# DMA transposes for q and k of batch 1 and for x of batches 2 and 3, and zero matmuls at the start, in a windowed-attention and gated-FFN kernel

## The chip, the cores and the metric

The kernel runs on one core of a Trainium2 chip. The metric is the device time of one execution in microseconds. Before the change the median of three runs is 214.59 us (213.76 to 214.88).

## The reference

Attention with a window of 128 and 4 sink keys for 4 batches of 8 heads, 768 positions and 64 elements per head. Its output, the heads side by side, is x (3072 tokens of 512), the input of a gated feed-forward part without a nonlinearity.

```python
scores = scale * np.matmul(q, k.transpose(0, 1, 3, 2))
is_sink = pos[None, :] < int(n_sink)            # n_sink 4
rel = pos[:, None] - pos[None, :]
in_window = (rel >= 0) & (rel < int(window))    # window 128
scores = np.where(is_sink | in_window, scores, -1000000000.0)
...
x = np.matmul(softmax(scores), v)    # then to 3072 x 512
a = x @ w1                           # 512 x 1024
b = x @ w2
h = a * b @ w3                       # 1024 x 1024
return (h @ w_out).astype(np.float32)   # 1024 x 512
```

## The kernel before, in words

**Attention.** A batch is cut into three stages t of 256 queries, and its 8 heads into four pairs r. For each batch q and k lie in SBUF with the tokens on the partitions (qN, kN) and must be transposed so that the head elements lie on the partitions (qT, kT). A batch has six key blocks kb of 128 tokens. `transposes` (L163) does two blocks with 8 TensorE transposes into one PSUM bank and one VectorE copy; `transposes_dma` (L175) does one block with one DMA transpose issued from SP. The set XPOSE (L54) says which batches take the second way: 2 and 3. `scores` (L216) makes the scores of one pair and stage (6 matmuls, or 4 for t = 0), ScalarE takes the exponential (L227), VectorE the mask (L231). `values` (L237) multiplies with v, and VectorE divides by the sum and writes xn (L259). `x_transposes` (L263) turns two pairs of xn into xT with 4 TensorE transposes and one ScalarE copy (L271).

**Feed-forward.** w3 and w_out are multiplied once (`fold_w3`, `fold_mm`, L297 to L317). `gate` (L277) makes a 128-column part of x @ w1 (half 0, copied out by ScalarE to a_sb) or of x @ w2 (half 1, multiplied by a_sb on VectorE into ab), 4 matmuls each, for a chunk of 256 tokens (batch 0) or 384 tokens (the others). `project` (L319) makes 128 rows of the result with 8 matmuls of 512 columns; ScalarE copies it to o_sb (L327), and SP issues the output (L330). The tile o_sb comes from the pool `work`, with 3 buffers.

**Queues.** All loads of inputs and weights are issued by POOL (L101, L104, L108) in the order of the list `order` (L124), with the type changed to bf16 on the way; for each batch and block k, q and v. SP issues the DMA transposes and the outputs. Each engine works through its own list in order. A load into a qN or kN buffer has to wait until that buffer's user of two batches before is done.

**Order.** TensorE, ScalarE, VectorE and SP have their order written out by a planner that runs while the kernel is built (L437 to L534). Tasks have stages (engine and assumed duration), predecessors (`after`), loads with assumed arrival times (L342) and a priority; `pe_pick` (L448) takes the task that can start first on TensorE, and the least priority number among those that needn't wait. The planner models the PSUM banks ("mm" with 4, "sc" with 2), but no buffer of the pool `work` and no sharing of the DMA engines: a DMA transpose is put at 1.4 us of SP and 6.5 us to landing (L381), an output at 0.1 us of SP (L433).

```python
task(qk[-1], 1, transposes_dma(src, dst, kb), [("sp", 1.4), ("dma", 6.5)],
     war, [(n, b, kb)])
```

Of the kernel before, what the change touches and what calls it, by code (L numbers as in the profile page):

```python
# [21 lines left out]
def kernel(  # L22
# [13 lines left out]
    nc = tc.nc  # L36
    FP32 = mybir.dt.float32
    BF16 = mybir.dt.bfloat16
# [4 lines left out]
    B, H, S, D = q.shape  # L43
    assert (B, H, S, D) == (4, 8, 768, 64)
    P = 128
    NP = H // 2
# [4 lines left out]
    KFF = DF // P  # L51

    CHUNKS = [[(256 * i, 256 * i + 256) for i in range(3)]] + [[(0, 384), (384, 768)]] * (B - 1)
    XPOSE = (2, 3)  # L54
    scale = 1.0 / float(D) ** 0.5

    const = ctx.enter_context(tc.tile_pool(name="const", bufs=1))
# [2 lines left out]
    work = ctx.enter_context(tc.tile_pool(name="work", bufs=3))  # L60
# [4 lines left out]
    ident = const.tile([P, P], BF16, name="ident")  # L65
# [5 lines left out]
    w3_sb = wp.tile([P, KFF, DF], BF16, name="w3_sb")  # L71
    wo_sb = wp.tile([P, KFF, DM], BF16, name="wo_sb")
    w3o = wp.tile([P, KFF, DM], BF16, name="w3o")
    VS = 80

    def per_batch(name, shape, bufs):
        return [inp.tile(shape, BF16, tag=f"{name}{b % bufs}", bufs=1, name=f"{name}_{b}")
# [48 lines left out]
             ("w3", 6, 8), ("qkv", 1, 0, 6), ("qkv", 2, 0, 6), ("qkv", 3, 0, 6)]  # L126

    nc.scalar.preload_act_table_set("natural_log_exp_and_others")
    nc.vector.memset(ident[:], 1.0)
    load(*order[0])  # L130
    nc.gpsimd.affine_select(ident[:], ident[:], compare_op=ALU.is_equal, fill=0.0,
# [24 lines left out]
    for x in order[4:]:  # L156
        load(*x)
    for b in range(B):
        nc.vector.memset(ksbd[b][:], 0.0)
        nc.vector.tensor_copy(vs[b][:, :, D], ones_s[:])  # L160


# [72 lines left out]
    xns = {}  # L235

    def values(b, r, t):  # L237

        am = ams.pop((b, r, t))
        av = ps_mm.tile([P, 2, 2, D + 1], FP32, tag="mm", name="av")  # L240
        todo = []
        for i in range(2):
            if t > 0:
                q0 = (t - 1) * 256 + i * P
                todo.append((av[:, i, :, :].rearrange("p e d -> p (e d)"), es[b][:, q0:q0 + P],
                             vs[b][:, 2 * r:2 * r + 2, :].rearrange("p e d -> p (e d)")))
            for kb, c in ((2 * t + i - 1, 2 * i * P), (2 * t + i, (2 * i + 1) * P)):
                if kb >= 0:
                    for e in range(2):
                        todo.append((av[:, i, e, :], am[:, e, c:c + P],  # L250
                                     vN[b][:, kb, 2 * r + e, 0:D + 1]))
        for n, (o, lhs, rhs) in enumerate(todo):
            nc.tensor.matmul(o, lhs, rhs, start=(n == 0), stop=(n == len(todo) - 1),  # L253
                             skip_group_check=True)
        yield
        rec = work.tile([P, 2, 2, 1], FP32, tag="rec", name="rec")
        nc.vector.reciprocal(rec[:], av[:, :, :, D:D + 1])  # L257
        xn = work.tile([P, 2, 2, D], BF16, tag="xn", bufs=4, name="xn")
        nc.vector.tensor_mul(xn[:], av[:, :, :, 0:D], rec[:].to_broadcast([P, 2, 2, D]))  # L259
        xns[b, r, t] = xn  # L260
        yield

    def x_transposes(b, r0, t):  # L263

        xt = ps_mm.tile([P, 2, 2, P], BF16, tag="mm", name="xt")
        for r in range(2):
            xn = xns.pop((b, r0 + r, t))
            for i in range(2):
                nc.tensor.transpose(xt[:, r, i, :], xn[:, i, :, :].rearrange("p e d -> p (e d)"), ident[:])  # L269
        yield  # L270
        nc.scalar.copy(xT[b][:, r0:r0 + 2, t * 256:(t + 1) * 256],  # L271
                       xt[:].rearrange("p r i m -> p r (i m)"))
        yield

    gate_a = {}
# [43 lines left out]
    def project(b, m):  # L319

        po = ps_mm.tile([P, DM], FP32, tag="mm", name="po")
        for kk in range(KFF):
            nc.tensor.matmul(po[:], ab[b][:, kk, m * P:(m + 1) * P], w3o[:, kk, :],  # L323
                             start=(kk == 0), stop=(kk == KFF - 1))
        yield
        o_sb = work.tile([P, DM], FP32, tag="o_sb", name="o_sb")
        nc.scalar.copy(o_sb[:], po[:])  # L327
        yield
        t0 = b * S + m * P
        nc.sync.dma_start(out=out[t0:t0 + P, :], in_=o_sb[:])  # L330
        yield


    arrive = {}
# [37 lines left out]
    for b in range(B):  # L372
        for t in range(NT):
            kbs = (2 * t, 2 * t + 1)
            qk = []
            war = [("av", b - 2, NP - 1, NT - 1)] if b >= 2 else []
            for n, src, dst in (("k", kN[b], kT[b]), ("q", qN[b], qT[b])):
                if b in XPOSE:
                    for kb in kbs:
                        qk.append(("tp" + n, b, kb))  # L380
                        task(qk[-1], 1, transposes_dma(src, dst, kb), [("sp", 1.4), ("dma", 6.5)],  # L381
                             war, [(n, b, kb)])
                else:
                    qk.append(("tp" + n, b, t))
                    task(qk[-1], 1, transposes(src, dst, t), [("pe", 0.48), ("dve", 0.62)],
                         war, [(n, b, kb) for kb in kbs], "mm")
            if t == 0:
                qk0 = qk
                task(("sk", b), 0, sink_keys(b), [("dve", 0.2)], [("sc", b, 1, 0)])
                task(("sv", b), 2, sink_values(b), [("pe", 0.3), ("act", 0.5)],  # L390
                     [("av", b - 2, NP - 1, NT - 1)] if b >= 2 else [], [("v", b, 0)], "mm")
            else:
                task(("ss", b, t), 2, sink_scores(b, t), [("pe", 0.5), ("act", 0.4)],
                     qk + [("sk", b)], ring="mm")
            for r in range(NP):
                after = list(qk)
                if b >= 2 and t == 0:
                    after.append(("g", b - 2, len(CHUNKS[b - 2]) - 1, KFF - 1, 1))
                lead = r % 2 == 0
                task(("sc", b, r, t), 4 if lead else 0, scores(b, r, t),  # L400
                     [("pe", 0.22), ("act", 0.83), ("dve", 0.58)] if t == 0 else
                     [("pe", 0.28), ("act", 1.05), ("dve", 0.7)], after, ring="sc",
                     slots=2 if lead else 1,
                     started=([("sc",) + unit[-1]] if unit else [])
                     + ([("av",) + unit[-3]] if lead and len(unit) > 3 else []))
                task(("av", b, r, t), 3, values(b, r, t),
                     [("pe", 0.2 if t == 0 else 0.37), ("dve", 0.55)],
                     [("sc", b, r, t)] + ([("ss", b, t), ("sv", b)] if t else []),
                     [("v", b, kb) for kb in kbs], "mm",
                     [("av",) + unit[-1]] if unit else [])  # L410
                unit.append((b, r, t))
                if not lead:
                    task(("xt", b, r - 1, t), 2.5, x_transposes(b, r - 1, t),
                         [("pe", 0.24), ("act", 0.6)],
                         [("av", b, r - 1, t), ("av", b, r, t)], [], "mm",
                         [("xt",) + unit[-4][:1] + (unit[-4][1],) + unit[-4][2:]] if len(unit) > 3 else [])
    gates = []
    for b in range(B):
        for c, (t0, t1) in enumerate(CHUNKS[b]):
            last_t = (t1 - 1) // 256  # L420
            us = 0.01 + 0.65 * (t1 - t0) / 384
            for dt in range(KFF):
                n = dt * P // 512
                pr = 1000 + 200 * b + 10 * c + dt
                war = [("p", b - 2, NB - 1)] if b >= 2 else []
                task(("g", b, c, dt, 0), pr + 0.5, gate(b, c, dt, 0), [("pe", us), ("act", 0.2 + us / 2)],
                     [("xt", b, NP - 2, last_t)] + war, [("w1", n), ("w2", n)], "mm",
                     [("g",) + gates[-2] + (1,)] if len(gates) > 1 else [])
                task(("g", b, c, dt, 1), pr, gate(b, c, dt, 1), [("pe", us), ("dve", 0.23 + us / 2)],
                     [("g", b, c, dt, 0)], ring="mm", half=True)  # L430
                gates.append((b, c, dt))
            for m in range(t0 // P, t1 // P):
                task(("p", b, m), 1300 + 200 * b + m, project(b, m), [("pe", 1.75), ("act", 0.6), ("sp", 0.1)],  # L433
                     [("g", b, c, KFF - 1, 1), ("fm", KFF - 1, 0), ("fm", KFF - 1, 1)], ring="mm")
# [4 lines left out]
    URGENT = {"g": 0, "av": 0, "sc": 2}  # L439
    PACE = 5.0  # L440
    last_sc = 0.0
    BACKLOG = 1.6
    free = {"pe": 0.0, "act": 0.0, "dve": 0.0, "sp": 0.0}
    rings = {n: [[0.0] for _ in range(k)] for n, k in (("mm", 4), ("sc", 2))}
# [54 lines left out]
    with tc.manual_schedule(engines={mybir.EngineType.PE, mybir.EngineType.Activation,  # L499
                                     mybir.EngineType.DVE, mybir.EngineType.SP}):  # L500
        while len(done) < len(tasks):
# [13 lines left out]
            start, _, e = min(moves)  # L515
            if e == "pe":
                k = pe[1]
                begun.add(k["name"])
                k["stage"] = 0
                us = k["stages"][0][1]  # L520
# [8 lines left out]
                queue[e].remove(q)  # L529
                us, k = q[2], q[3]  # L530
            next(k["gen"])
            if e == "pe" and start - free[e] > 0.3: print("model idle", k["name"], round(start,2), round(start - free[e],2))
            free[e] = start + us
            advance(k, free[e])  # L534

# [33 lines left out]
```

The softmax here doesn't subtract the row's maximum and nothing guards it: scores larger than these inputs give would overflow.

## Time and profile before

| | |
|---|---|
| median of three runs | 214.59 us |
| the profiled execution | 214.53 us |
| its span, first to last instruction | 212.8 us |
| TensorE busy | 195.3 us, 92% |
| VectorE, ScalarE busy | 109.5 us, 110.4 us |
| POOL busy (issuing loads) | 75.0 us, the last load issued at 98.5 us |
| mean granted TensorE clock | 0.989 |
| chain that ended last | PE 86%, POOL 5%, DMA 3%, DVE 3% |
| gate matmuls (L284) in that chain | 41% |
| projections (L323) in that chain | 20% |
| TensorE transposes (L168 and L269) in that chain | 4% |

A share of busy time is a mean over the whole span. The start, to about 27 us, has idle TensorE while weights and the first batch arrive; the middle, to about 117 us, has TensorE and the DMA engines both full; after that the DMA engines carry little but the outputs. The chain lists, followed back from the last instruction, what each step waited for. The prediction below quotes the lines it rests on: slices, the chain in order of time, and the timelines of POOL and SP, whose columns are the start in us, the time taken in us, the engine, the line, the operation, what it writes and reads, and in brackets what it waited for.

### The profile page before, as it was taken

Reading aid. Unit: us, or ns where it says so; the run is one execution under the profiler, and the core shown is the slowest. Engines: PE = TensorE matmul, PEld = TensorE weight load, DVE = VectorE, ACT = ScalarE, POOL = GpSimd, SP = SyncE. Lnnn points to the kernel's source line nnn. Section 1 sums busy time; section 2 is a strip of 40 time slices with the busy share of each in tenths; the row PEclk is TensorE's granted clock in tenths of the full one; section 3 lists DMA queues with packets and bytes.
Section 4 is the critical chain, followed back from the end, with each engine's and each line's share of the span. In section 5 each row is a group of like instructions: output and inputs, shape, how many; then the busy total and the mean of one; then the engine's idle time right before and its main releaser. Section 6 shows DMA issues by size and latency. Waiting matters only on the chain.

```text
span 212.8 us, 4647 instructions
## 1 busy us (share of the span) xinstructions
PE 195.3 (92%) x1888; PEld 131.8 (62%) x1888; DVE 109.5 (51%) x258; ACT 110.4 (52%) x197; POOL 75.0 (35%) x97
## 2 busy tenths in 40 slices
PE   0287799999998999999999999999999999999993
PEld 0266468998987887666666555666664466554441
DVE  7116825836697787776776444687740044440000
ACT  2012636644866686786666766766643333323332
POOL 7996573679999665666000000000000000000000
PEclk9999969999999999999999999999999999999998
DMA  4999999999999999999996222100002310002343
GB/s 65 160 170 205 165 198 204 163 178 157 156 155 132 156 156 149 136 154 146 140 117 124 102 107 93 49 2 3 0 3 99 148 49 3 2 0 99 152 162 133
DMA packets 96710, 24.43 MB, mean 115 GB/s; under 512 B 88496, under 2 KB 92592, under 8 KB 96688
## 3 DMA queue, kind: packets, MB, share of 16 engines
q0 software_dynamic: 80176, 14.69, 89.5%
q1 hardware_dynamic: 16512, 9.44, 21.3%
q8 instruction: 15, 0.25, 0.5%
q14 instruction: 7, 0.06, 0.1%
HBM read 29.36 MB, written 6.29 MB: 168 GB/s over the span
## 4 chain that ended last, share of the span: by engine, by line
PE 86%; POOL 5%; DMA 3%; DVE 3%; issue 1%; ACT 1%; POOLq 0%; ACTq 0%; DVEq 0%
PE pg L284 41%; PE po L323 20%; PE av L253 7%; PE sc L222 6%; PE pw L313 6%; DMA w_sb<-in_moe_w_dram 3%; PE xt L269 3%; PE sp L202 2%; PE tp L168 1%; POOL vN_90 L101 1%; POOL qN_82 L101 1%; DVE xn L259 1%; POOL kN_86 L101 1%; DVE am L231 1%; POOL w_sb L108 1%
## 5 line engine op out<-in xcount | busy, mean ns | idle before, releaser
L284 PEld LDWEIGHTS <-w_sb 128*128 128x128 bf16 x576 | 54.2, 99 | 27.6 <-issue 3.4
L227 ACT ACTIVATE ex<-sc 128x1024 bf16<-128x1024 f32 (+1 forms) x48 | 44.3, 955 | 13.3 <-PE sc L222 13.0
L291 ACT COPY a_sb<-pg 128x384 f32<-128x384 f32 (+1 forms) x72 | 32.1, 446 | 34.2 <-PE pg L284 20.0
L231 DVE TENSOR_TENSOR am<-ex,maskt 128x1024 bf16<-128x1024 bf16 (+1 forms) x48 | 30.4, 643 | 10.0 <-ACT ex L227 9.0
L327 ACT COPY o_sb<-po 128x512 f32<-128x512 f32 x24 | 14.0, 585 | 27.2 <-PE po L323 24.8
L284 PE MATMUL pg<-xT_102,w_sb 128*128 128x256 bf16 x192 | 26.6, 285 | 1.1 <-DVE kT_99 L171 0.6
L284 PE MATMUL pg<-xT_103,w_sb 128*128 128x384 bf16 x128 | 23.8, 326 | 0.0
L284 PE MATMUL pg<-xT_104,w_sb 128*128 128x384 bf16 x128 | 23.0, 326 | 0.0
L313 PE MATMUL pw<-wo_sb,w3t 128*128 128x256 bf16 x128 | 17.3, 291 | 4.6 <-DMA wo_sb<-in_moe_w_out_dram 3.8
L259 DVE TENSOR_TENSOR xn<-av,rec 128x256 bf16<-128x256 f32 x48 | 20.4, 425 | 1.7
L284 PE MATMUL pg<-xT_105,w_sb 128*128 128x384 bf16 x128 | 21.0, 326 | 0.0
L288 DVE TENSOR_TENSOR ab_109<-a_sb,pg 128x384 bf16<-128x384 f32 x16 | 8.9, 555 | 22.3 <-PE pg L284 22.3
L253 PEld LDWEIGHTS <-am 128*128 128x128 bf16 x352 | 16.7, 97 | 2.9 <-DVE am L231 1.1
L313 PEld LDWEIGHTS <-w3t 128*128 128x128 bf16 x128 | 12.5, 103 | 7.4 <-issue 3.1
L257 DVE RECIPROCAL rec<-av 128x4 f32<-128x4 f32 x48 | 8.6, 179 | 14.9 <-PE av L253 14.8
L316 ACT CAST w3o<-pw 128x256 bf16<-128x256 f32 x16 | 5.8, 379 | 18.0 <-PE pw L313 17.9
L288 DVE TENSOR_TENSOR ab_106<-a_sb,pg 128x256 bf16<-128x256 f32 x24 | 10.0, 417 | 9.7 <-PE pg L284 9.7
L288 DVE TENSOR_TENSOR ab_108<-a_sb,pg 128x384 bf16<-128x384 f32 x16 | 8.8, 552 | 5.8 <-PE pg L284 5.4
L323 PE MATMUL po<-w3o,ab_106 128*128 128x512 bf16 x48 | 11.4, 380 | 0.0
L269 PE MATMUL xt<-ident,xn 128*128 128x128 bf16 x96 | 9.7, 220 | 1.2 <-DVE xn L259 1.2
L323 PE MATMUL po<-w3o,ab_107 128*128 128x512 bf16 x48 | 10.7, 379 | 0.0
L323 PE MATMUL po<-w3o,ab_108 128*128 128x512 bf16 x48 | 10.7, 379 | 0.0
(129 smaller groups left out, 261.3 us busy)
## 6 DMA issues: line engine op xcount, KB each, us to landing
out_dram<-o_sb SPq DMA_DIRECT2D x24, 256.0 KB, 2.0
w_sb<-in_moe_w_dram POOLq DMA_DIRECT2D x7, 512.0 KB, 9.8
wo_sb<-in_moe_w_out_dram POOLq DMA_DIRECT2D x2, 512.0 KB, 8.8
kN_86<-in_k_dram POOLq DMA_DIRECT2D x6, 128.0 KB, 10.8
qN_82<-in_q_dram POOLq DMA_DIRECT2D x6, 128.0 KB, 10.7
vN_90<-in_v_dram POOLq DMA_DIRECT2D x6, 128.0 KB, 9.9
kN_87<-in_k_dram POOLq DMA_DIRECT2D x6, 128.0 KB, 7.2
qN_83<-in_q_dram POOLq DMA_DIRECT2D x6, 128.0 KB, 6.6
```

The lines of the kernel that those rows point to most:

```text
L222: nc.tensor.matmul(sc[:, e, c:c + n], kT[b][hp, r, kb * P:(kb + 1) * P], qT[b][hp, r, qb * P:qb * P + n], start=True, stop=True)
L227: nc.scalar.activation(ex[:, :, c0:], sc[:, :, c0:], ACTF.Exp, scale=scale)
L231: nc.vector.tensor_mul(am[:, :, c0:], ex[:, :, c0:], mk)
L253: nc.tensor.matmul(o, lhs, rhs, start=(n == 0), stop=(n == len(todo) - 1), skip_group_check=True)
L259: nc.vector.tensor_mul(xn[:], av[:, :, :, 0:D], rec[:].to_broadcast([P, 2, 2, D]))
L269: nc.tensor.transpose(xt[:, r, i, :], xn[:, i, :, :].rearrange("p e d -> p (e d)"), ident[:])
L284: nc.tensor.matmul(pg[:], w_sb[:, kk, dt * P:(dt + 1) * P], xT[b][:, kk, tk], start=(kk == 0), stop=(kk == NP - 1))
L288: nc.vector.tensor_mul(ab[b][:, dt, tk], gate_a.pop((b, c, dt))[:], pg[:])
L291: nc.scalar.copy(a_sb[:], pg[:])
L313: nc.tensor.matmul(po[:], w3T[i][:, j, :], wo_sb[:, j, cols], start=(j == 0), stop=(j == KFF - 1))
L323: nc.tensor.matmul(po[:], ab[b][:, kk, m * P:(m + 1) * P], w3o[:, kk, :], start=(kk == 0), stop=(kk == KFF - 1))
L327: nc.scalar.copy(o_sb[:], po[:])
```

## The change

Four things are altered.

1. Batch 1 joins the set XPOSE: its q and k are transposed by 12 DMA transposes from SP instead of 48 TensorE transposes in six groups with a VectorE copy each.
2. For batches 2 and 3 (X_XPOSE) xn is transposed by DMA: `x_transposes_dma` takes one 128-token block of all heads, two per stage, 12 in all, from SP. xn becomes one tile for all four pairs of a stage, with 2 buffers instead of 4 smaller ones. The gates of these batches wait for the two DMA transposes of their chunk's last stage.
3. `keep_busy`: where the planner sees TensorE idle for over 0.5 us before its own 40 us, it puts matmuls of a zeroed tile there (ksbd of batch 3), 512 columns each; nothing reads what they write.
4. The pitch of v's rows in SBUF (VS) goes from 80 to 72 elements.

Since the planner runs anew, the order of all four engines changes. In the new order TensorE has 1888 - 96 + 50 = 1842 matmuls: 40 of the 50 zero matmuls stand ahead of the third transposed block of w3, 10 between the first values and the first gates. All 48 gate groups of batch 0 come before the second score stage of batch 1 (31 of them did), and the six projections of batch 0, which stood around the end of batch 2's attention, now stand between the second and the third score stage of batch 1 and beside them. On SP their outputs stand among the transposes of batch 2:

```
kT_100 qT_96 kT_100 qT_96 kT_100 qT_96 kT_100     (blocks 0 to 3)
out 0   qT_96 kT_100   out 1   qT_96 kT_100   out 2   qT_96   out 3  out 4  out 5
12 transposes of kT_101 and qT_97
4 transposes of xT_104   2 outputs   2 of xT_104   4 of xT_105   3 outputs   2 of xT_105
13 outputs
```

On POOL batch 2 now begins with two loads of v, and batch 3 goes k, q, v by block, where its six loads of v came first before; the first loads of k and q of batch 3 wait until all 12 transposes of batch 1 have landed.

```diff
-    XPOSE = (2, 3)
+    XPOSE = (1, 2, 3)
+    X_XPOSE = (2, 3)
...
-    VS = 80
+    VS = 72
...
+    idle = ksbd[B - 1]
+    nc.vector.memset(idle[:], 0.0)
...
-        xn = work.tile([P, 2, 2, D], BF16, tag="xn", bufs=4, name="xn")
-        nc.vector.tensor_mul(xn[:], av[:, :, :, 0:D], rec[:].to_broadcast([P, 2, 2, D]))
-        xns[b, r, t] = xn
+        if r == 0:
+            xns[b, t] = work.tile([P, 2, NP, 2, D], BF16, tag="xn", bufs=2, name="xn")
+        nc.vector.tensor_mul(xns[b, t][:, :, r, :, :], av[:, :, :, 0:D],
+                             rec[:].to_broadcast([P, 2, 2, D]))
...
+    def x_transposes_dma(b, t, i):
+
+        q0 = t * 256 + i * P
+        nc.sync.dma_start_transpose(out=xT[b][:, :, q0:q0 + P],
+                                    in_=xns[b, t][:, i].rearrange("p r e d -> p (r e d)"))
+        yield
...
+    def keep_busy(n):
+
+        pz = ps_mm.tile([P, 512], FP32, tag="mm", name="pz")
+        for _ in range(n):
+            nc.tensor.matmul(pz[:], idle[:, 0:P], idle[:, 0:512], start=True, stop=True)
...
+            if b in X_XPOSE:
+                for i in range(2):
+                    task(("xd", b, t, i), 1, x_transposes_dma(b, t, i), [("sp", 1.3), ("dma", 4.0)],
+                         [("av", b, NP - 1, t)])
...
-                     [("xt", b, NP - 2, last_t)] + war, [("w1", n), ("w2", n)], "mm",
+                     ([("xd", b, last_t, 0), ("xd", b, last_t, 1)] if b in X_XPOSE else
+                      [("xt", b, NP - 2, last_t)]) + war, [("w1", n), ("w2", n)], "mm",
...
+    START, WARM_UNTIL = 1.2, 40.0
...
+                gap = start - max(free["pe"], START)
+                if gap > 0.5 and start < WARM_UNTIL and rings["mm"][0][0] is not None \
+                        and rings["mm"][0][0] <= max(free["pe"], START):
+                    keep_busy(int((gap - 0.25) / 0.22))
+                    rings["mm"] = rings["mm"][1:] + [[max(free["pe"], START)]]
```

More of the change, by code (lines that the diff above doesn't have):

```diff
@@ L158 @@
     for b in range(B):
-        nc.vector.memset(ksbd[b][:], 0.0)
+        if b < B - 1:
+            nc.vector.memset(ksbd[b][:], 0.0)
         nc.vector.tensor_copy(vs[b][:, :, D], ones_s[:])
@@ L266, in x_transposes @@
         for r in range(2):
-            xn = xns.pop((b, r0 + r, t))
             for i in range(2):
-                nc.tensor.transpose(xt[:, r, i, :], xn[:, i, :, :].rearrange("p e d -> p (e d)"), ident[:])
+                nc.tensor.transpose(xt[:, r, i, :],
+                                    xns[b, t][:, i, r0 + r, :, :].rearrange("p e d -> p (e d)"),
+                                    ident[:])
         yield
@@ L411 @@
                 unit.append((b, r, t))
-                if not lead:
+                if not lead and b not in X_XPOSE:
                     task(("xt", b, r - 1, t), 2.5, x_transposes(b, r - 1, t),
                          [("pe", 0.24), ("act", 0.6)],
-                         [("av", b, r - 1, t), ("av", b, r, t)], [], "mm",
-                         [("xt",) + unit[-4][:1] + (unit[-4][1],) + unit[-4][2:]] if len(unit) > 3 else [])
+                         [("av", b, r - 1, t), ("av", b, r, t)], [], "mm")
+            if b in X_XPOSE:
+                for i in range(2):
+                    task(("xd", b, t, i), 1, x_transposes_dma(b, t, i), [("sp", 1.3), ("dma", 4.0)],
+                         [("av", b, NP - 1, t)])
     gates = []
@@ L531 @@
             next(k["gen"])
-            if e == "pe" and start - free[e] > 0.3: print("model idle", k["name"], round(start,2), round(start - free[e],2))
             free[e] = start + us
```

## The prediction

> **What bounds the kernel now.** I read the page's slices first, then the chain of waits, then the timelines of SP and POOL, because the change moves work from TensorE to the DMA engines.
>
> ```profile
> PE   0287799999998999999999999999999999999993
> ...
> PEclk9999969999999999999999999999999999999998
> DMA  4999999999999999999996222100002310002343
> ```
>
> One slice is 5.3 us. TensorE is full from about 27 us to the end. The DMA engines are full too, from the start to about 117 us (22 slices), and nearly idle afterwards. So there are two full resources in the first half and one in the second. The chain in order of time shows what the removed work costs, and one slow stretch:
>
> ```profile
> 27.02 5.12 PE pg L284 x30
> ...
> 44.56 0.22 PE xt L269 x4
> 44.78 3.93 PE pg L284 x36
> 48.71 0.45 PE tp L168 x8
> ```
>
> 30 gate matmuls at 27.02 take 171 ns each, 36 of the same shape at 44.78 take 109 ns: the first stretch runs in the one slice whose clock digit is 6. Eight transposes cost 0.45 us, four cost 0.22. Now the queues, POOL (loads) and SP (DMA transposes and outputs):
>
> ```profile
> 39.40 0.90 POOL L101 DMA_DIRECT2D kN_87<-in_k_dram  x1 [1.51 <-DMA w_sb<-in_moe_w_dram]
> ...
> 55.93 0.94 POOL L101 DMA_DIRECT2D vN_91<-in_v_dram  x1
> ...
> 57.57 0.88 POOL L101 DMA_DIRECT2D kN_88<-in_k_dram  x1 [0.39 <-PE pw L313]
> 63.43 1.31 SPq L177 DMA_TRANSPOSE kT_100<-kN_88  x1
> ...
> 74.21 1.19 SPq L177 DMA_TRANSPOSE kT_100<-kN_88  x1
> 75.44 1.27 SPq L177 DMA_TRANSPOSE qT_96<-qN_84  x1
> 78.84 1.19 SPq L177 DMA_TRANSPOSE kT_100<-kN_88  x1
> 80.70 1.19 SPq L177 DMA_TRANSPOSE qT_96<-qN_84  x1
> 83.67 1.19 SPq L177 DMA_TRANSPOSE kT_100<-kN_88  x1
> ...
> 114.65 1.22 SPq L177 DMA_TRANSPOSE qT_97<-qN_85  x1
> 116.89 93.37 SPq L330 DMA_DIRECT2D out_dram<-o_sb  x24
> DMA to landing us min/median/max: 7.2/7.5/7.9
> DMA to landing us min/median/max: 2.5/7.1/8.3
> out_dram<-o_sb SPq DMA_DIRECT2D x24, 256.0 KB, 2.0
> ```
>
> The first two landing lines are those of kT_100 and kT_101 in the views by tile. A transpose starts when its load has landed. Batch 1, with no transposes beside it, is issued at one load per 0.87 us. In batch 2 a block (three loads, two transposes) takes 4.6 to 4.8 us (74.21, 78.84, 83.67) where three loads alone take 2.6. All 24 outputs come after the last transpose, when the DMA engines are free, and land in 2.0 us.
>
> [...]
>
> **The change part by part.** I write "projection m" for the six 128-row output blocks of batch 0.
>
> TensorE, removed: 48 transposes of q and k of batch 1, 6 x 0.45 = 2.7 us; 48 of x of batches 2 and 3, 12 x 0.22 = 2.6 us. DVE loses six 0.69 us copies and ACT twelve 0.59 us copies; neither is the bound.
>
> Zero matmuls: 50 of 512 columns. A projection (8 of 512) takes 1.73 us, so 0.22 each at full clock, 0.43 at half. 40 stand before the third transposed block of w3, which waits for its load until 18.76; with the first 11 and the first block's 8 transposes at half clock and the rest at full, they and the real work end at about 17 to 18 us, so cost nothing; were the clock late they cost up to 2 us, and below nothing they can't gain there, since the load decides. The last 10 stand in the gaps between 20 and 27 us and gain 30 x (171 - 109) = 1.9 us if the clock holds, nothing if not. I take 1.9. With nothing else the sum is -2.7 - 2.6 - 1.9 = -7.2.
>
> DMA, added: 12 transposes of batch 1, among loads. Price of one: from 63.43 to 83.67 stand 15 loads (13.05) and 10 transposes in 20.24 us, 0.72 each; from 74.21 to 83.67, 6 loads (5.2) and 4 transposes in 9.46, 1.06 each. I take 0.9. So every load of batch 2 lands 12 x 0.9 = 10.8 us later. (The 12 of x come after the loads and cost the loads nothing.) The pitch of v, 144 bytes for 160, costs 0: k at 128 and v at 160 are equally fast in the trace; the range allows for worse.
>
> Moved: the planner brings the projections of batch 0 forward, from 114.5 us to between the second and third stage of batch 1's scores, and their outputs stand between batch 2's transposes on SP: after k block 3 output 0, after k block 4 output 1, after k block 5 output 2. When does TensorE come there? Batch 1's second score stage starts at 70.75 now. Ahead of it in the new order stand 17 more gate matmul groups (x 0.437 = 7.4), six fewer transpose groups (-2.7) and one small group (0.3): +5.0, less 1.9 of clock: 73.9. Projection 3 then stands 7.9 us further, at 81.8, projection 5 at 86.8, done at 88.5.
>
> But their copies (ACT) write o_sb, which has 3 buffers: projection 3 needs output 0 landed, projection 5 output 2. Output 2 waits behind k block 5: 83.67 + 10.8 + 2 x 0.7 for the outputs ahead (between 0.3 and 1.8 each: free while others move, or twice a transpose, for twice the bytes) + 1.25 issue = 97.1. It lands 2.0 us later if free, 7.4 later like the transposes ahead of it in its queue: 99.1 to 104.5; I take 101.5, nearer the middle than either. ACT is in order, so all exponentials and gate copies queue behind the waiting copy, and "mm" has 4 PSUM banks: the x transpose four groups after projection 5 needs its bank. TensorE goes on at 101.5 + 0.6 (copy) + 0.1.
>
> What remains from there, in the new order: 95 gate groups x 0.65 (384 columns) = 61.8; 18 projections x 1.735 = 31.2; 18 value groups x 0.36 and 8 x 0.18 = 7.9; scores 16 x 0.275 + 8 x 0.22 = 6.2; sinks and two x transposes 2.5: 109.6. Idle in the same part now: (209.3 - 70.75, from the chain) less 136.4 of work at the same prices = 2.2; I take 1.5. End of TensorE: 102.2 + 109.6 + 1.5 = 213.3, against 209.3 now: +4.0.
>
> A second constraint gives nearly the same. x of batch 2 is queued on SP behind batch 3's transposes. Their last, now at 114.65, moves by 10.8 + 6 outputs x 0.7 - 1.8 (POOL's idle at 85 to 90, used now): 127.9. Four x transposes at 1.25 follow, landing 2.5 later: about 134.5. The first gate group of batch 2 waits for it, and 77.6 us of work (64 gate groups, 16 projections, the rest of batch 3) remain: 212.8 with 0.7 idle. So a bigger o_sb alone would not bring the gain.
>
> TensorE's hole between 84 and 102 us can also cost a stretch at half clock, 0 to 1.9 us; I take 0.5, since part is hidden by the second wait. Sum: +4.5 on the profiled execution's 214.53 (span 212.8 and 1.7 around it; the median of the runs is 214.59): **219.0**.
>
> **Rivals.** *A, forecast*: outputs stuck behind transposes among loads, 213 to 223. At a price of 0.72, 0.3 for an output and landing in 2.0 us, output 2 lands at 96.1 and TensorE ends at 207.9: 213.1.
>
> *B, worse in the same place*: price 1.06, output 1.8, landing 7.4: output 2 lands at 108.6, TensorE ends at 220.4[...]: 224 to 229, take 226. For: 4.7 us blocks at the end of batch 2. Against: the mean of 0.72.
>
> *C, faster*: the outputs slip through. If a transpose costs 0.5 of load time, an output 0.3, and outputs land in 2.0 us, output 2 lands at 93.5 (end 205.3) and x of batch 2 at 128.2, where TensorE with its whole gain would come at 123.4: the 7.2 shrink to 2.4. Near a price of 0 nothing waits: 207.3 to 212.1, take 210. For: DMA time may be spare in batch 1, whose issue rate is POOL's own 0.87. Against: loads land 7 us after issue, so a backlog stands. It decides below about 0.6 us per transpose.
>
> *D, even*: stalls of 12 us eat the 7.2 and the slack exactly: 214.5.
>
> **How the numbers follow.** Chances: A 0.52, B 0.20, C 0.17, D 0.11. A measurement tells about 0.5% (1.1 us) from no change. A lies above 215.6 but for a small tail that I count with D. So slower 0.72, same 0.11, faster 0.17. The range 211 to 225 leaves out the better half of C and the worse half of B.
>
> **What would show it.** Right: ACT's o_sb copies waiting for an out transfer at 84 to 102 us; TensorE's slices there falling to 4 to 7; SP's out entries between transposes; batch 2's first gates waiting for xT; load blocks of 4.4 us in batch 1; clock digit 9 at 27 us. Wrong: TensorE full through 80 to 105 us, or kN_88's last load landing before 90 us. If the o_sb copies don't wait but the time is longer, the x transposes are the cause.

## The result, and the profile after

| | before | after |
|---|---|---|
| median of four runs | 214.74 us (213.76 to 216.41) | 224.53 us (222.58 to 226.62) |
| ratio after/before | | 1.042, 95% interval 1.031 to 1.053 |
| span of the profiled execution | 212.8 us | 224.9 us |
| TensorE busy | 195.3 us | 203.0 us, of which the zero matmuls 14.7 (48 of the 50 are in the trace) |

The medians of all runs differ by 9.8 us; the ratio, which leaves out the slow one of after's four runs (226.62 us), puts the cost at 4.2% (interval 3.1 to 5.3), about 9.0 us. The profiled execution of after is that longest run, so its last instructions stand 2 us later than the median's; of the other three there is no trace.

The slices of after (one slice is 5.6 us; a digit is the busy share in tenths, for the clock the granted share):

```profile
PE   7698889999997499829699999999999999999993
...
PEclk9999999999999679976699999999999999999999
DMA  5999999999999999999999997220202360001333
```

TensorE starts early (the zeros) and then has two holes, in slices 12 and 13 (67 to 79 us) and 16 to 19 (90 to 112 us, the digits 8, 2, 9, 6), with clock digits of 6 and 7 in or just behind each. DMA is full for 24 slices of 5.6 us, to 135 us, where it was 22 of 5.3, to 117 us. In the chain that ended last DMA has 39% of the span, where it had 3%: from 13.5 us to the second hole it runs through the landings of seven loads, one after the other. The chain in order of time, from the last of these loads on (start, us taken, what):

```profile
86.85 13.51 DMA kN_88<-in_k_dram
...
100.37 1.26 SPq L181
...
101.72 6.39 DMA out_dram<-o_sb
...
108.21 0.59 ACT o_sb L340
...
108.85 0.58 PE xt L273 x4
109.44 2.56 PE pg L297 x8
...
115.27 1.41 PE pg L297 x8
```

That is the forecast's sequence: a load, a DMA transpose on SP, the output behind it, its landing, the copy into o_sb, TensorE. The first eight gate matmuls take 2.56 us, later ones 1.41: the clock digit is 6 in that slice, and the granted clock 0.50 from 109.44 to 112.00 us. SP's entries left in the order of its list: the copies of the first three outputs ended at 85.03, 87.77 and 90.51 us on ScalarE, and the outputs left at 90.78, 95.44 and 101.72, each behind the transposes ahead of it. SP's timeline:

```profile
78.97 1.20 SPq L181 DMA_TRANSPOSE kT_100<-kN_88  x1
...
89.38 1.32 SPq L181 DMA_TRANSPOSE kT_100<-kN_88  x1
90.78 0.56 SPq L343 DMA_DIRECT2D out_dram<-o_sb  x1
...
94.11 1.23 SPq L181 DMA_TRANSPOSE kT_100<-kN_88  x1
95.44 0.56 SPq L343 DMA_DIRECT2D out_dram<-o_sb  x1
...
100.37 1.26 SPq L181 DMA_TRANSPOSE kT_100<-kN_88  x1
101.72 0.53 SPq L343 DMA_DIRECT2D out_dram<-o_sb  x1
```

The first transpose of batch 2 comes at 78.97, where it was 63.43; the last of k at 100.37, where it was 83.67. So 15.5 of the 16.7 us of lateness are there when batch 2's transposes begin, before the first output leaves at 90.78. They arise in the loads. On POOL's timeline after, the last k load of batch 1 waits for an earlier load to land, and the first of batch 2 for a buffer that TensorE still reads:

```profile
58.99 0.88 POOL L102 DMA_DIRECT2D kN_87<-in_k_dram  x1 [2.41 <-DMA qN_83<-in_q_dram]
...
68.09 0.88 POOL L102 DMA_DIRECT2D kN_88<-in_k_dram  x1 [0.88 <-PE pg L297]
```

and the first of these two before:

```profile
54.20 0.92 POOL L101 DMA_DIRECT2D kN_87<-in_k_dram  x1
```

The second was issued at 57.57 then. On ScalarE's timeline the three copies that waited for outputs, in brackets how long and for what:

```profile
98.96 0.59 ACT L340 COPY o_sb<-po 128x512 f32<-128x512 f32 x1 [7.97 <-DMA out_dram<-o_sb]
...
102.96 0.59 ACT L340 COPY o_sb<-po 128x512 f32<-128x512 f32 x1 [1.57 <-DMA out_dram<-o_sb]
...
108.21 0.59 ACT L340 COPY o_sb<-po 128x512 f32<-128x512 f32 x1 [4.18 <-DMA out_dram<-o_sb]
```

And TensorE's own timeline before them, the first hole, which the forecast did not have:

```profile
72.83 0.60 PE L206 MATMUL sp<-qT_95,ksbd_111 128*128 128x256 bf16 x4 [1.42 <-DMA qT_95<-qN_83]
77.22 0.61 PE L196 MATMUL vp<-vN_92,sel 128*128 128x64 bf16 x8 [3.36 <-DMA vN_92<-in_v_dram]
```

Here TensorE waits for the loads and transposes directly, without an output between: for the fourth q block of batch 1 and then for the first v of batch 2. That is 4.8 us of waiting. In the second hole the waits add up to 7.1 us (in total, times, longest):

```profile
PE xt L273 <- ACT o_sb L340: 7.1, 2, 4.7
```

After each of the two longest waits TensorE works slowly for a while: 16 gate matmuls from 78.05 take 3.61 us, 226 ns each, where 109 ns is usual (granted clock 0.52 over them), and 8 matmuls of a projection from 99.98 take 3.62, where 1.73 is usual (granted clock 0.50).

### The profile page after: what moved, and what is told of

Its sections match the earlier page's. It is cut to its first block, busy times and chain, and to the rows that moved or that the text cites. A ratio compares the mean times of both kernels' runs of the same rounds, so it can differ in the third digit from the quotient of the medians.

```text
span 224.9 us, 4580 instructions
## 1 busy us (share of the span) xinstructions
PE 203.0 (90%) x1832; PEld 131.8 (59%) x1842; DVE 107.1 (48%) x252; ACT 104.7 (47%) x185; POOL 75.2 (33%) x97
## 4 chain that ended last, share of the span: by engine, by line
PE 50%; DMA 39%; POOL 6%; issue 2%; SPq 1%; ACT 1%; POOLq 0%; ACTq 0%
PE pg L297 29%; DMA w_sb<-in_moe_w_dram 15%; PE po L336 14%; DMA kN_87<-in_k_dram 6%; DMA kN_88<-in_k_dram 6%; DMA qN_84<-in_q_dram 5%; DMA qN_83<-in_q_dram 4%; PE av L257 4%; DMA out_dram<-o_sb 3%; PE sc L226 3%; POOL w_sb L109 1%; POOL vN_90 L102 1%; POOL qN_82 L102 1%; PE sp L206 1%; POOL kN_86 L102 1%
## 5 line engine op out<-in xcount | busy, mean ns | idle before, releaser
L297 PEld LDWEIGHTS <-w_sb 128*128 128x128 bf16 x576 | 55.1, 100 | 27.1 <-issue 2.8
L297 PE MATMUL pg<-xT_102,w_sb 128*128 128x256 bf16 x192 | 24.9, 285 | 0.0
L297 PE MATMUL pg<-xT_103,w_sb 128*128 128x384 bf16 x128 | 24.7, 339 | 0.0
L297 PE MATMUL pg<-xT_104,w_sb 128*128 128x384 bf16 x128 | 23.1, 326 | 0.0
L297 PE MATMUL pg<-xT_105,w_sb 128*128 128x384 bf16 x128 | 21.0, 326 | 0.0
L257 PEld LDWEIGHTS <-am 128*128 128x128 bf16 x352 | 17.8, 100 | 3.6 <-DVE am L235 0.5
L326 PE MATMUL pw<-wo_sb,w3t 128*128 128x256 bf16 x128 | 15.7, 273 | 3.3 <-DMA wo_sb<-in_moe_w_out_dram 3.1
L350 PE MATMUL pz<-ksbd_113 128*128 128x512 bf16 x48 | 14.7, 437 | 1.4 <-DVE ksbd_113 L131 1.3
L326 PEld LDWEIGHTS <-w3t 128*128 128x128 bf16 x128 | 11.8, 98 | 6.0 <-issue 2.5
L336 PE MATMUL po<-w3o,ab_106 128*128 128x512 bf16 x45 | 12.9, 424 | 0.2
L273 PE MATMUL xt<-ident,xn 128*128 128x128 bf16 x48 | 5.6, 240 | 7.6 <-ACT o_sb L340 7.1
L336 PE MATMUL po<-w3o,ab_107 128*128 128x512 bf16 x45 | 11.0, 379 | 0.2
```

The source lines that it names most:

```text
L297: nc.tensor.matmul(pg[:], w_sb[:, kk, dt * P:(dt + 1) * P], xT[b][:, kk, tk], start=(kk == 0), stop=(kk == NP - 1))
L326: nc.tensor.matmul(po[:], w3T[i][:, j, :], wo_sb[:, j, cols], start=(j == 0), stop=(j == KFF - 1))
L350: nc.tensor.matmul(pz[:], idle[:, 0:P], idle[:, 0:512], start=True, stop=True)
```

## The experiments

Two theories stood against each other. *Queue*: the outputs of batch 0, caught between transposes on SP, are the cause; free them and most of the 10 us come back. *Lateness*: each transpose of batch 1 makes all later loads and transposes late, and the output wait is only the wait in front; take it away and another takes its place.

All times are medians; each stands beside runs of the kernel before on the same chip (215.6 us for the first four, 214.97 for the next four, 215.18 for the last three). The chips differ between these groups, so runs of different groups are best compared by their ratios.

| run | us | ratio to before, 95% interval |
|---|---|---|
| after, with 8 o_sb buffers | 223.68 | 1.034, 1.025 to 1.043 |
| x by DMA, zeros | 216.73 | 1.007, 1.003 to 1.011 |
| q and k of batch 1 by DMA, zeros | 229.92 (224.99 to 230.61) | none taken |
| zeros alone | 216.24 | 1.003, 1.000 to 1.005 |
| after, without zeros | 224.83 | 1.045, 1.039 to 1.050 |
| x by DMA alone | 215.81 | 1.000, 0.998 to 1.003 |
| pitch of v alone | 215.39 | 1.001, 0.998 to 1.003 |
| x of batch 3 alone | 214.58 | 0.998, 0.995 to 1.000 |
| after, outputs issued by ScalarE | 222.48 | 1.035, 1.030 to 1.040 |
| k of batch 1, x of batch 3 | 219.27 | 1.018, 1.013 to 1.023 |
| x by DMA alone, three xn tiles | 214.44 | 0.996, 0.993 to 0.998 |

**Eight output buffers.** On after; outputs are staged in w3_sb, which is free by then:

```diff
-        o_sb = work.tile([P, DM], FP32, tag="o_sb", name="o_sb")
+        o_sb = w3_sb[:, (b * NB + m) % KFF, :].bitcast(FP32)
```

> The changed kernel, but the outputs are staged in eight buffers (the eight blocks of w3, dead by then) instead of three. Theory 1 (the three o_sb buffers behind the blocked SP queue are the cause): the 13.7 us of ACT's o_sb copies waiting for outputs go and the time falls by about 12 us, to 211 to 214. Theory 2 (the loads and transposes themselves are late, the buffers are only where it shows first): the stall moves to TensorE waiting for v of batch 3 (L196) and for xT of batch 2 (L297), which land no earlier than 101 and 137 us; with 77.6 us of work after the latter the time stays at 217 to 221.

223.68, about 0.9 us below after, with wide intervals; neither theory had this time (211 to 214, and 217 to 221). No copy waits for an output any more. Its waits instead (us in total, times, longest):

```profile
DVE xn L264 <- DMA xT<-xn: 6.1, 1, 6.1
PE vp L196 <- DMA vN<-in_v_dram: 5.4, 2, 3.0
PE pg L297 <- DMA xT<-xn: 3.3, 1, 3.3
```

TensorE waits for v twice, and batch 2's gates for the transposed x, as the forecast's "second constraint" said. The output wait was in front of others. That speaks for *lateness*.

**The parts.** On after, with only the lists changed, while the pitch of v and the larger xn tile of all batches stay and the planner orders each version anew:

```diff
 x by DMA, zeros:                    XPOSE = (2, 3)
 q and k of batch 1 by DMA, zeros:   X_XPOSE = ()
 zeros alone:                        XPOSE = (2, 3); X_XPOSE = ()
```

> The changed kernel with batch 1's q and k back on TensorE; x of batches 2 and 3 by DMA and the zero matmuls stay. If the 12 transposes of batch 1 are what costs, all of the loss goes and 2.6 + 1.9 us are gained: 210 us, outputs of batch 0 again behind all transposes of q and k, no wait of o_sb copies. If x by DMA costs (SP queue, two xn tiles), it stays at or above 214.5 and TensorE waits at L297 for xT.

> The changed kernel with x of batches 2 and 3 back on TensorE; batch 1 by DMA and the zero matmuls stay. If batch 1's transposes and the outputs among them are the cause, the whole loss is here too, plus 2.6 us of TensorE transposes: 224 to 228. If the x transposes on SP matter, it is 4 us or more faster than the changed kernel: 220 or less.

> Only the zero matmuls and v's pitch of 72; all transposes as before. If the half-clock stretch at 27 us costs what its matmuls show, the 30 gate matmuls take 3.3 us instead of 5.1 and the time falls by 1.9 to 212.8. If the gain is lost in a later wait for loads, or the zero matmuls are in the way, or v's pitch slows the loads, it stays at 214 to 216.

The loss is in batch 1's transposes: with them back on TensorE the ratio falls from 1.042 to 1.007, and with nothing but them and the zeros even the quickest of four runs takes 224.99 (the median of 229.92 comes from runs that spread too far for a comparison). But the other parts don't gain what I had expected. With x by DMA, TensorE stands before the sink scores of batch 2's third stage, in its timeline:

```profile
97.33 0.60 PE L206 MATMUL sp<-qT,ksbd 128*128 128x256 bf16 x4 [2.94 <-DMA qT<-qN]
```

In before these four matmuls start at about 93.7 us; the last q block that they read was issued at 84.95 and took 7.6 us to land, so it had been there for 1.1 us (the expectations below put this at 0.9). So a gain ahead of 93 us is worth about 1 us at most, unless the loads come earlier too: behind it stands the DMA supply. With zeros alone TensorE's timeline shows why the zeros gained nothing:

```profile
15.73 3.19 PE L350 MATMUL pz<-ksbd 128*128 128x512 bf16 x13
18.76 0.40 PE L196 MATMUL vp<-vN,sel 128*128 128x64 bf16 x8
...
20.10 1.06 PE L314 MATMUL tp<-ident,w_sb 128*128 128x128 bf16 x16
...
27.79 0.81 PE L350 MATMUL pz<-ksbd 128*128 128x512 bf16 x3
28.44 3.66 PE L297 MATMUL pg<-xT,w_sb 128*128 128x256 bf16 x32
```

and the same work in before:

```profile
15.11 0.63 PE L192 MATMUL vp<-vN_90,sel 128*128 128x64 bf16 x8
...
18.76 0.62 PE L301 MATMUL tp_304<-ident,w_sb 128*128 128x128 bf16 x8 [1.45 <-DMA w_sb<-in_moe_w_dram]
...
27.02 5.10 PE L284 MATMUL pg<-xT_102,w_sb 128*128 128x256 bf16 x30 [0.46 <-ACT xT_102 L271]
```

The gates do run at full clock (32 in 3.66 us, where 30 took 5.10; in after, whose 32 took 3.66 too, the granted clock over them is 1.00), but they start 1.4 us later and end at the same time, 32.1. Thirteen zeros stand ahead of vp, which ran at 15.11 in before, and push it to 18.76: the zeros stood not only where TensorE had to wait, but ahead of ready work.

**Without zeros; x alone; pitch; x of batch 3 alone.** The first two take the zeros out of after and of "x by DMA"; the third changes one number of before (VS from 80 to 72); the fourth is the second with batch 3 only:

```diff
-    START, WARM_UNTIL = 1.2, 40.0
+    START, WARM_UNTIL = 1.2, 0.0
```

> The changed kernel without its 48 zero matmuls; all three groups of transposes and the 72-element pitch of v stay. If the zero matmuls only warm the clock (my prediction), the gates of 27 us go back from 109 to 171 ns, but the end hangs on the third output's landing, so the time moves by 0 to +1: 224 to 226. If instead they push work ahead of the loads back and make POOL's load queue late (first load of batch 1's k at 41.6 us in the changed kernel, 39.4 before), leaving them out brings that load to about 39.5 us and everything behind it 1 to 2 us earlier: 222 to 223.5.

> Only x of batches 2 and 3 is transposed by the DMA engines; q and k of batch 1 stay on TensorE and there are no zero matmuls (pitch of v 72). If the 32 x transposes come off TensorE free, 2.6 us go: 212. If the gain ahead of 93 us is lost because the sink scores of batch 2 wait for the last DMA transpose of q (0.9 us of slack before), batch 2's x counts for nothing and batch 3's 1.3 us remain, or are lost to VectorE waiting for the x transposes: 213.3 to 216.

> The kernel before with nothing but the pitch of v's rows at 72 instead of 80 elements. If the pitch is free (my prediction): 214.6, and the first load of batch 1's k is at 39.4 us as before. If the pitch is what makes the loads late in all variants so far: 215.6 to 216.5, and that load at 40.4 us or later.

> As the run with x alone, but for batch 3 only: 16 transposes fewer on TensorE, all after 93 us. If they come off the path: 1.3 us less, 213.3. If VectorE's two xn tiles wait for the DMA transposes, or gates for xT: 214.6 to 215.6.

The pitch is free (ratio 1.001). Its trace shows more: it has before's order of instructions, and its 30 gates at 27 us took 3.44 us without any zero matmul, at full clock (granted 0.998 over that whole execution). TensorE then came to batch 2's sink scores 1.3 us earlier than in before, at 91.95, and waited there for the last q block. Its timeline:

```profile
27.12 3.44 PE L284 MATMUL pg<-xT,w_sb 128*128 128x256 bf16 x30 [0.46 <-ACT xT L271]
...
94.24 0.60 PE L202 MATMUL sp<-qT,ksbd 128*128 128x256 bf16 x4 [1.69 <-DMA qT<-qN]
```

So the slow stretch at 27 us (in before, granted clock 0.67 over the 5.10 us) is not in every execution, and this one, where it is missing, took no less (215.04 us, the profiled one of before 214.53): with the 1.9 us gone that the zeros were to remove, TensorE only came to this wait for the DMA supply.

Without zeros the loads are earlier, as the second theory of that expectation said (batch 1's first k load at 39.92 instead of 41.63 us), but the time is not: the third output leaves at 100.34 instead of 101.72 and takes 7.99 us to land, in the chain of the run without zeros:

```profile
100.34 7.99 DMA out_dram<-o_sb
```

It lands at 108.33, where after's lands at 108.11. x alone takes 48 transposes off TensorE and x of batch 3 alone 24 (not 32 and 16, as expected above). x alone saves TensorE 4.0 us of busy time (191.3 against 195.3), of which 1.7 are the gates at 28 us, which ran at full clock here too (3.43 for 30), and gives no gain. Its waits, and the place in SP's timeline:

```profile
DVE xn L264 <- DMA xT<-xn: 5.3, 1, 5.3
```

```profile
113.52 1.22 SPq L181 DMA_TRANSPOSE qT<-qN  x1
114.84 5.13 SPq L284 DMA_TRANSPOSE xT<-xn  x4
```

The transposes of x of batch 2 stand behind the last of batch 3's q and k, so both xn tiles stay taken until 118.6 us, VectorE waits, and TensorE idles 1.7 us for it. x of batch 3 alone has no such wait; its ratio of 0.998 is on the edge of what can be told from no change, against the 1.3 us that were expected.

**Outputs from ScalarE's queue, on after:**

```diff
-        nc.sync.dma_start(out=out[t0:t0 + P, :], in_=o_sb[:])
+        nc.scalar.dma_start(out=out[t0:t0 + P, :], in_=o_sb[:])
```

> The changed kernel with the 24 output DMAs issued from ScalarE's queue instead of SP's; nothing else. If the outputs' place on SP behind the DMA transposes is what costs (the working of my prediction), the first outputs leave 5 us earlier, the third wait for o_sb goes and the end comes at 219 to 220. If the loads themselves are late and the o_sb wait only stood in front of other waits (as with eight o_sb buffers, 223.7), it stays at 222 to 224.5.

222.48, a ratio of 1.035 against 1.042, so some 1.5 to 2 us of after's loss may be the outputs' place on SP (the intervals overlap). It is not the clean test that I meant: ScalarE's timeline shows the first output leaving at 93.13, later than on SP (90.78), after a wait for a transpose:

```profile
93.13 0.38 ACTq L343 DMA_DIRECT2D out_dram<-o_sb  x1
93.56 0.59 ACT L340 COPY o_sb<-po 128x512 f32<-128x512 f32 x1 [8.08 <-DMA kT<-kN]
```

Why the output on ScalarE's queue was held until a transpose of k had landed was not tried. What the run does show: the last k transpose of batch 2 is at 98.44 with no output before it on SP, still 14.8 us later than in before, and the outputs still take up to 7.4 us to land.

**Half the transposes of batch 1** (k only; x of batch 3 only, no zeros):

```diff
-                if b in XPOSE:
+                if b in XPOSE and (b, n) != (1, "q"):
```

> Of batch 1 only k is transposed by the DMA engines (6 instead of 12), of x only batch 3's, no zero matmuls: to be set against the run with x of batch 3 alone (214.6). If each DMA transpose of batch 1 costs the load queue 0.9 us as I predicted: 5.4 us of lateness, less 0.9 us of slack before batch 2's sink scores, less 1.3 us of TensorE time: 217.8. At 1.2 us each: 219.5. If the loss only begins when the outputs get caught behind the transposes (a threshold): 214 to 215.5.

219.27, near the value for 1.2 us each, and no threshold. With it there are three pairs whose edits differ in nothing but batch 1's transposes (the planner then orders each anew). From SP's timelines, the start of batch 2's first transpose:

| pair | transposes added | first transpose of batch 2, us | each | time, us | each |
|---|---|---|---|---|---|
| x of batch 3 alone; with k of batch 1 | 6 | 64.28; 71.19 | 1.15 | 214.58; 219.27 | 0.78 |
| x alone; after without zeros | 12 | 63.83; 76.86 | 1.09 | 215.81; 224.83 | 0.75 |
| x with zeros; after | 12 | 66.65; 78.97 | 1.03 | 216.73; 224.53 | 0.65 |

So each DMA transpose of batch 1 makes what follows 1.03 to 1.15 us later, and 0.65 to 0.78 us of that reach the end (0.63 to 0.79 by the ratios), though each also takes 0.22 us of transposing off TensorE. Not all of it need be the transfer itself: POOL waits up to 1.3 us for a buffer that TensorE still reads before it issues batch 2's first k load; if that wait counts in full, 0.95 to 1.02 are left. The lateness stands before any output of batch 0 leaves (86.70 us at the earliest in these runs), so it does not come from the outputs, and with eight buffers the loss stayed: that decides for *lateness*. What share of the end time is the outputs' is not measured, since in all three pairs the planner also moves them among the transposes; no run has batch 1's transposes with before's order. In the half run an output wait is in front as well; in its chain:

```profile
90.50 7.84 DMA out_dram<-o_sb
```

**Three xn tiles, on x alone** (and one tile `rec` instead of three, to make room):

```diff
-            xns[b, t] = work.tile([P, 2, NP, 2, D], BF16, tag="xn", bufs=2, name="xn")
+            xns[b, t] = work.tile([P, 2, NP, 2, D], BF16, tag="xn", bufs=3, name="xn")
```

> The run with x alone (q, k of batch 1 on TensorE, no zero matmuls; 215.8) with three xn tiles instead of two (and one rec tile instead of three, to make room). If VectorE's wait for the DMA transposes of x of batch 2, which stand on SP behind the last transposes of batch 3 (5.3 us, of which TensorE idles 1.7), is what ate the gain: 213.5 to 214. If the gates of batch 2 then wait for the same transposes instead: no change, 215 to 216.

214.44: 0.4% below before (0.2 to 0.7), 0.7 us by the medians, a little less than the 213.5 to 214 expected, and the only version whose interval lies below 1. VectorE's wait is gone. What is left of TensorE's waits for DMA behind the start is that for the last q of batch 2, in its timeline, and it is again the DMA supply:

```profile
94.53 0.60 PE L206 MATMUL sp<-qT,ksbd 128*128 128x256 bf16 x4 [1.35 <-DMA qT<-qN]
```

## Why the prediction was right, and where its sizes were off

The direction, the place and the chain were as written: ScalarE's o_sb copies wait for outputs from 90 to 108 us, the outputs stand behind k blocks 3, 4 and 5, and TensorE's busy digits fall to 2 there. One sign named did not come: batch 2's first gates did not wait for xT. The size was far off. 224.53 is inside the range, near its end, 5.5 us above the forecast; the loss is 9.8 us by the medians (9.0 by the ratio), where 4.4 was forecast. That is outside A's own 213 to 223 and inside B's 224 to 229, which had a chance of 0.20, and output 2 landed at 108.11, where B had 108.6: it is the width given for B that keeps the number in the range, not the sum. Three corrections below (4.6, 2.0 and 1.0), all in one direction, make up the 7.6 us by which the profiled execution, 226.62, lies above 219.0. Step by step:

- **A transpose of batch 1, taken as 0.9 us (0.72 to 1.06).** Measured by the three pairs: 1.03 to 1.15, or 0.95 to 1.02 without POOL's wait for a buffer, so near the upper bound or above it. I let the mean over all five blocks (0.72) pull down what the last two showed (1.06). Both take the 0.87 us at which POOL issues as the price of a load; why the early blocks look cheaper was not tried. Twelve cost 12.3 us of lateness in after, not 10.8.
- **Zero matmuls, "cost nothing", gaining 1.9.** They gained nothing and made the loads late: with them batch 2's first transpose is at 66.65 (x with zeros) and 66.91 (zeros alone), in the five traces with neither zeros nor batch 1's transposes at 63.43 to 64.50. How they do it was not tried. "x with zeros" and "x alone" differ only in them, and the last k transpose of batch 2 is at 86.85 against 83.87; in after and "after, without zeros" it is at 100.37 against 98.99. So the sum lacked 1.4 to 3 us here. The 1.9 was the slow stretch of one execution, read as the kernel's; in the pitch run it was missing, and the time was no better. I had compared the end of the zeros with the load of w3's third block, and not looked at what stands between (vp and the transposes of batch 0). In after the end hung on the output's landing, and they cost nothing that can be measured (224.83 without). The price of a single one was about right: the first 11 of after took 4.88 us and the next ten 2.32, 0.44 and 0.23 each, where 0.43 at half clock and 0.22 at full were taken (the granted clock reads 1.00 in both stretches).
- **Outputs at 0.7 each.** With the outputs on ScalarE's queue batch 2's first transpose stands where it does in after (78.96 and 78.97), and k block 5's at 98.44 instead of 100.37: 1.0 each, inside the 0.3 to 1.8 allowed.
- **Landing, taken at 4.4 us between 2.0 and 7.4.** It was 6.4, and 7.99 and 7.84 in two other runs: the outputs among loads and transposes took about as long to land as the transposes there (8.1, 7.5 and 6.4 us for the first three of after, 7.0 to 9.3 for the six of batch 2's k). The 2.0 us of before came from the time after 117 us, where the DMA share is 0.18, and should have had little weight.
- **Output 2 issued at 97.1, TensorE again at 102.2.** It was 101.72 and 108.85: 4.6 from the first three terms together, 2.0 from landing.
- **Remaining work, 109.6 + 1.5 idle, and 0.5 for half clock.** TensorE ended at 221.4, 112.6 after it resumed. With the 0.5 counted, 1.0 was lacking. The first two gate groups after the hole alone took 2.56 where 1.41 is usual, 1.15 of slow clock (granted 0.50) where 0.5 was allowed for all. The two stretches before cost 1.87 (16 gates from 78.05) and 1.89 us (8 matmuls from 99.98); B's 224 to 229, for a TensorE that ends at 220.4, left room for such stretches, by an estimate of mine.
- **The second constraint, "a bigger o_sb alone would not bring the gain".** Right: eight buffers end at 223.68. Its sum was 0.9 short: 127.9, four transposes of 1.25 and a landing of 2.5 make 135.4, not 134.5. In after itself batch 2's x did not bind, because TensorE came later than the forecast had it.
- **TensorE's 7.2 us of removed work.** The zeros' 1.9 did not come. The 2.7 of batch 1 lie ahead of waits for DMA and shorten nothing. Of the 2.6 of x, 0.7 remain even in the best version, since batch 2's first half is bound by DMA with about 1 us to spare.
- **Not foreseen:** the first hole, with its waits for q of batch 1 (1.4 us) and for v of batch 2 at 74 to 77 us (3.4 us). I had followed the outputs and x, but not each load that TensorE reads directly.

## What to carry to other kernels

Here the transposes moved from TensorE to DMA were paid in lateness of what stood behind them in the load stream, 1.03 to 1.15 us for each of batch 1. Before moving such work, find the first instruction on TensorE that waits for that stream and how long its operand has been there; here it was about 1 us, against 12. Price a transfer from the most loaded stretch of the trace, not from a mean and never from idle stretches, and count the landing of outputs that share the time the same way (6.4 us here, where idle stretches showed 2.0). Put filler work only where nothing ready stands behind it in the same list: thirteen zeros moved vp from 15.11 to 18.76 us. A slow stretch of the clock in one trace is not yet a cost of the kernel (30 gates took 5.10 us in before and 3.44 in the pitch run): look for it in a second execution, and at what waits behind it.

## What the runs showed of the hardware

- A DMA transpose of a 128x512 bf16 tile among loads made what stood behind it 1.03 to 1.15 us later (0.95 to 1.02 without POOL's wait for a buffer), by the three pairs above. What it takes of the DMA engines when they have little else to do can be set beside an output. The views of DMA (packets, MB, and the time that the packets took as a share of 16 engines) of 133 to 158 us in "x alone", with 6 transposes, and of 120 to 212 us in before, with 23 outputs by their bytes, say:

```profile
q1 hardware_dynamic: 3264, 0.79, 16.6%
q1 hardware_dynamic: 3312, 6.03, 17.0%
```

So by this estimate (16.6% of 25 us by 6, 17.0% of 92 us by 23) a transpose of 128 KB takes 0.69 us of all 16 engines and an output of 256 KB 0.68: per byte the transpose took twice as long. The two are not alike in all else, since the output leaves SBUF and the transpose stays in it.
- An output of 256 KB landed 2.0 us after its issue in before, behind the last load and transpose (median of 24, at most 2.8), and 5.9 to 8.1 us after it among loads and transposes in after. From ScalarE's queue, among them too, it took 6.1 to 7.4.
- The speed of the gates of 27 us differs between executions. In the seven traces without zero matmuls 30 of these gates took 5.1 us in three (170 ns each) and 3.43 to 3.44 us in four (114 ns); in all six with zeros 32 took 3.66 us (114 ns). Whether the zeros bring the full clock, six against seven executions don't show. In the same list they took as long as they saved: with zeros alone the gates end at 32.1 us, as in before.
